# One-bank running sums, one decay tile per chunk, a later conversion of the first weights, and plain float32 second products for four pairs of the first tile

## The chip, the cores and the metric

The kernel runs on one core of a Trainium2 chip. The core has TensorE (PE in the profile; its weight loads are shown as PEld), VectorE (DVE), ScalarE (ACT), GpSimd (POOL) and SyncE (SP), which issues all DMAs here. The metric is the device time of one execution in microseconds; lower is better. A kernel's time is the median of its runs.

## The reference

Four sequences of 768 positions and 8 heads go through a state-space layer (chunks, a decaying state of 16 per head), and its output, 3072 tokens of 256 values, through two feed-forward layers:

```
for c in range(nc):                                  # chunks; cum = cumsum(log a)
    M = einsum(Cc, Bc) * exp(cum_i - cum_j) * causal
    y[c] = M @ xc + (Cc @ state) * exp(cum)
    state = exp(sum(la)) * state + sum_j Bx_j * exp(cum_last - cum_j)
x = y.transpose(0, 2, 1, 3).reshape(3072, 256)
h = x @ w_in                                         # 256 -> 2048
x = where(h > 0, h, exp(min(h, 0)) - 1) @ w_out      # 2048 -> 256
out = ((x @ w1) * (x @ w2)) @ w3 @ w_out2            # 256 -> 1024 -> 1024 -> 256
```

All is float32; the weights arrive as 64-bit words, of which the kernel makes float32 values.

## The kernel before, in words

**Tiles and units.** The 3072 tokens are six tiles of 512 (`t` = 0 to 5), each made of four chunks of 128 positions. For each tile there are 8 units `a` (`unit_a(t, n)`: the product `h` with `w_in`, two 512-column halves in one two-bank tile, then ELU on ACT and DVE, then a split into a rounded part and a remainder, `g`), 8 units `b` (`unit_b(t, n)`: `g` with `w_out`, summed over n in a tile `acc`), 8 units `c` (products with `w1` and `w2`, `ab`, multiplied on DVE into `p`) and 8 units `d` (`p` with `wp`, summed in `acc`). `wp` is w3 times the last weight, made once by 8 units `w`.

**Split products.** A product in full precision is three rounded products (float32r): `mm3` (lines 240 to 242) issues weight-remainder times value, weight times value-remainder, and weight times value. So each operand is held twice, and each value that feeds a product has a split (`split`, lines 103 and 104: a cast on ACT, a subtraction on DVE or POOL). The small products of the state-space chunks (lines 351, 387, 416, 422) use plain float32 operands; each of them stands in the trace as two MATMUL instructions.

**Pieces of weights.** `w_in` and `w_out` come in 8 pieces each. A piece has three stages: load (a DMA on SP's queue), bits (lines 146 to 148: two DVE instructions and one ACT instruction make float32 of the words, in place), parts (lines 103 and 104: the split into the stationary operands). The queue of pieces follows the order of the units that need them: entry 0 is `w_in`'s piece 0, then pieces 1 and 2, then entry 3 is `w_out`'s piece 0, and so on.

**Order.** The four chunks of tile 0 come first, each in four phases: prep (a scan on DVE, line 334, of the decay values that `at_wide` spreads over partitions by a product with a 0/1 matrix, line 321, then `bd` on POOL), cb (products and their decay, lines 351 and 359), state (cd on POOL, products line 387, states on DVE lines 396 and 399) and y (lines 416, 422, then x_made, lines 431 and 432). The list `ORDER` gives their order by hand: phase p of chunk k is number 4k + p; "pr" is a scan of the decays in another layout (lines 261 to 303), "aw" the second `at_wide`, "h" the first half of the columns of unit a(0, 0), and (i, s) takes entry i of the queue to stage s. The chunks of later tiles are set between the units of the tile before by a plan. Within the dependencies a scheduler at build time then fixes the order of each engine's instructions; every engine works through its own list in order.

**Rooms.** PSUM has eight banks of 512 float32. The pool `ps_w` has three rooms of two banks, `ps_a` one room of two banks, which holds `acc` (and `aw2` before). `xx` in SBUF has three rooms for each part of the tiles `xT` (input of a) and `x2` (output of b, input of c). x2 of tiles 0 to 2 is stored to DRAM and read back.

Of the kernel before, what the change touches and what calls it, by code (L numbers as in the profile page):

```python
# [7 lines left out]
F32 = mybir.dt.float32  # L8
F32R = mybir.dt.float32r
AF = mybir.ActivationFunctionType  # L10
ALU = mybir.AluOpType
# [8 lines left out]
TT = 512  # L20
NTILE = NB * S // TT
CPT = TT // Q
DM = NH * D
F1 = 2048
F2 = 1024
# [8 lines left out]
PACE, FOLD, LATE, END, FIRST = 1.5, 4.0, 12.0, 7.0, 8.0  # L34
SPILL, BACK = 3, 8

ORDER = [0, 4, 1, "pr", 2, "aw", (0, 2), 5, 3, 6, (0, 3), 8, 7, 9, (1, 2), 10, 12, 11, 13, (1, 3), 14, "h", 15, (2, 2), (3, 2)]


XCOLS = (("x", DM), ("bn", NH * N), ("bt", 2 * R), ("cz", 2 * 2 * R), ("cp", SUB * 2 * R))  # L40
# [3 lines left out]
def kernel(  # L44
# [21 lines left out]
    P = 128  # L66
# [35 lines left out]
    def split(hi, lo, raw, lo_eng):  # L102
        A.copy(hi, raw)  # L103
        return lo_eng.tensor_tensor(out=lo, in0=raw, in1=hi.bitcast(F32), op=ALU.subtract)  # L104

    def tmp(name):
        return act.tile([P, 2, TT], F32, tag="tmp", name=name, bufs=TMP)

    def banks(name):

        return ps_w.tile([P, 2, TT], F32, tag="w", name=name)
# [9 lines left out]
    class Piece:  # L121


        def __init__(self, name, src, room, dst):
            self.name, self.src, self.room, self.dst = name, src, room, dst
            self.done, self.lo = 0, G

        def advance(self, stage):
            while self.done < stage:
# [11 lines left out]
        def bits(self):  # L141

            low, high = self.low, self.high
            pace(V.tensor_scalar(low, low, 29, None, op0=ALU.logical_shift_right))
            pace(A.activation(high.bitcast(F32), high.bitcast(F32), AF.Prelu, scale=2.0 ** -112, alpha=2.0 ** 32))
            V.scalar_tensor_tensor(out=low, in0=high, scalar=3, in1=low,
                                   op0=ALU.logical_shift_left, op1=ALU.bitwise_or)

        def parts(self):
            hi, lo = self.dst()
            word = self.low.bitcast(F32)
            if isinstance(hi, list):
                for k in range(2):
                    split(hi[k], lo[k], word[:, k], self.lo)
            else:
                split(hi, lo, word, self.lo)
# [45 lines left out]
    def rows_of(ws):  # L204
        return lambda i: [w[:, 2 * i:2 * i + 2] for w in ws]

    def four(name, tag, shape):
        t = [wts.tile(shape, F32R, tag=f"{tag}_{j}", name=f"{name}_{j}") for j in range(4)]
        return [t[:2], t[2:]]
# [13 lines left out]
    def w3_dst(i):  # L223
# [9 lines left out]
        "w1": pieces_of("wa", cols(w1), w1_room, half_cols(w1_s, "w1")),  # L233
        "w2": pieces_of("wb", cols(w2), w2_room, half_cols(w2_s, "w2")),
    }

    last_mm = []

    def mm3(out, whi, wlo, xhi, xlo, first, last, **kw):
        last_mm[:] = [T.matmul(out, wlo, xhi, start=first, stop=False, **kw).ins]  # L240
        T.matmul(out, whi, xlo, start=False, stop=False, **kw)  # L241
        T.matmul(out, whi, xhi, start=False, stop=last, **kw)  # L242
# [72 lines left out]
    def at_wide(k):  # L315


        wide = ps_a.tile([P, 2, TT], F32, tag="acc", name=f"aw{k}") if k else banks(f"aw{k}")
        for j in range(2):
            for p in range(2):  # L320
                mm = T.matmul(wide[:, j], sel[:, k + j].rearrange("r s i -> r (s i)"),
                              cut[0][:, p].rearrange("r h i -> r (h i)"), start=p == 0, stop=p == 1)
                if j == p == 0:
                    tc.keep_in_program_order(mm)
            ck[k + j]["a"] = wide[:, j]

    def at_prep(k):

# [170 lines left out]

    early_h = []  # L500

    def products(h, t, n, cs):
        for j in range(2):
            fs = slice((2 * n + j) * P, (2 * n + j + 1) * P)
            for k in range(2):
                mm3(h[:, j, cs], w_in_s[0][:, k, fs], w_in_s[1][:, k, fs], xT[t][0][:, k, cs], xT[t][1][:, k, cs],
                    k == 0, k == 1)

    def first_half():

        early_h.append(banks("h0_0"))
        products(early_h[0], 0, 0, slice(0, TT // 2))

    def unit_a(t, n):

        early = early_h and (t, n) == (0, 0)
        h = early_h[0] if early else banks(f"h{t}_{n}")
        products(h, t, n, slice(TT // 2 if early else 0, TT))
        e = tmp(f"e{t}_{n}")
        A.activation(e, h, AF.Exp)  # L520

        A.activation(e, e, AF.Relu, scale=-1.0, bias=1.0)  # L522
        V.scalar_tensor_tensor(out=e, in0=e, scalar=-1.0, in1=h, op0=ALU.mult, op1=ALU.max)  # L523
        g = act.tile([P, 2, 2, TT], F32R, tag="g", name=f"g{t}_{n}")
        split(g[:, 0], g[:, 1], e, V)
        gt[t, n] = g

    def acc_of(key):
        if key not in accs:
            accs[key] = ps_a.tile([P, 2, TT], F32, tag="acc", name=f"acc_{key[0]}{key[1]}")  # L530
        return accs[key]

    def unit_b(t, n):
        acc = acc_of(("b", t))
        g = gt.pop((t, n))

        for i in range(2):
            es = slice(i * P, (i + 1) * P)
            for j in range(2):
                m = 2 * n + j  # L540
                mm3(acc[:, i], w_out_s[0][:, m, es], w_out_s[1][:, m, es], g[:, 0, j], g[:, 1, j], m == 0, m == F1 // P - 1)
        if m == F1 // P - 1:
            hi, lo = x2_of(t)
            for i in range(2):
                split(hi[:, i], lo[:, i], acc[:, i], V)
            if t < SPILL:
                for v, d in zip(x2.pop(t), x2_dram):
                    nc.sync.dma_start(d[t], v.bitcast(F32))

    x2_dram = [tc.dram_tile([SPILL, P, 2, TT], F32, name=f"x2_dram{p}") for p in ("h", "l")]  # L550

    def x2_of(t):
        if t not in x2:
            x2[t] = [act.tile([P, 2, TT], F32R, tag=f"xx{p}", name=f"x2{p}{t}", bufs=3) for p in ("h", "l")]
        return x2[t]
# [22 lines left out]
    def unit_d(t, m):  # L578
        acc = acc_of(("d", t))
        p = pt.pop((t, m))  # L580
        for i in range(2):
            es = slice(i * P, (i + 1) * P)
            mm3(acc[:, i], wp_s[0][:, m, es], wp_s[1][:, m, es], p[:, 0], p[:, 1], m == 0, m == F2 // P - 1)
        if m == F2 // P - 1:
            o = [tmp(f"o{t}")] * 2 if t < NTILE - 1 else [tmp(f"o{t}_{i}") for i in range(2)]
            A.copy(o[0][:, 0], acc[:, 0])
            V.tensor_copy(o[1][:, 1], acc[:, 1])
            for i in range(2):
                nc.sync.dma_start(outT[i * P:(i + 1) * P, t * TT:(t + 1) * TT], o[i][:, i])


    NA, NC = F1 // P // 2, F2 // P
# [124 lines left out]
        p.advance(1)  # L717
    for k in range(CPT):
        at_l(k)
    at_wide(0)  # L720
    for p in queue[:first_n]:
        p.lo = V

    for j in ORDER:
        if j == "pr":
            at_decay(0)
        elif j == "aw":
            at_wide(2)
        elif j == "h":
            first_half()  # L730
        elif isinstance(j, tuple):
            i, stage = j
            queue[i].advance(stage)
            if stage == 3:
                load_next(i)
        else:
            attn[j]()
            marks.extend(last_mm)
# [72 lines left out]
```

## Time and profile before

| | |
|---|---|
| time, median of 3 runs | 571.41 us (571.39 to 571.74) |
| the profiled execution's own time | 570.61 us |
| its span in the profile | 568.7 us |
| PE busy | 550.6 us, 97% of the span, 4436 matmuls |
| PE weight loads | 440.3 us, 77% |
| DVE busy | 337.0 us, 59% |
| ACT busy | 274.2 us, 48% |
| POOL busy | 85.8 us, 15% |

Busy time is the time in which at least one instruction of the engine was under way. Matmuls overlap (one starts before the one ahead of it has drained), so a stretch can be wholly busy and still hold fewer matmuls than it could: distances between starts tell more than the busy share. The shares are averages over stages that differ: the state-space chunks of tile 0 fill the first 28 us, the conversion of the first weights runs beside tile 0's units until about 76 us, and dense products fill the rest.

### The profile page before, as it was taken

Reading aid. Unit: us, or ns where it says so; the run is one execution under the profiler, and the core shown is the slowest. Engines: PE = TensorE matmul, PEld = TensorE weight load, DVE = VectorE, ACT = ScalarE, POOL = GpSimd, SP = SyncE. Lnnn points to the kernel's source line nnn. Section 1 sums busy time; section 2 is a strip of 40 time slices with the busy share of each in tenths; the row PEclk is TensorE's granted clock in tenths of the full one; section 3 lists DMA queues with packets and bytes.
Section 4 is the critical chain, followed back from the end, with each engine's and each line's share of the span. In section 5 each row is a group of like instructions: output and inputs, shape, how many; then the busy total and the mean of one; then the engine's idle time right before and its main releaser. Section 6 shows DMA issues by size and latency. Waiting matters only on the chain.

```text
span 568.7 us, 10514 instructions
## 1 busy us (share of the span) xinstructions
PE 550.6 (97%) x4436; PEld 440.3 (77%) x4436; DVE 337.0 (59%) x480; ACT 274.2 (48%) x378; POOL 85.8 (15%) x91
## 2 busy tenths in 40 slices
PE   5998999999999999999999999999999999999996
PEld 3676677878788888878787878877878878888785
DVE  6599987867878674757425434243766353344342
ACT  2297567567745566764214222223644452365232
POOL 2201112430333432351000000000111000000000
PEclk9999999999999999999999999999999999999999
DMA  8978352553434341640001511021000000010001
GB/s 289 324 254 242 133 165 80 168 183 112 149 111 150 131 157 67 222 136 12 0 1 39 192 50 56 2 93 56 37 20 2 2 1 0 1 37 0 1 0 38
DMA packets 27167, 52.78 MB, mean 93 GB/s; under 512 B 2192, under 2 KB 10384, under 8 KB 27120
## 3 DMA queue, kind: packets, MB, share of 16 engines
q1 hardware_dynamic: 27120, 52.11, 28.3%
q8 instruction: 35, 0.57, 0.4%
q14 instruction: 12, 0.10, 0.1%
HBM read 45.71 MB, written 6.39 MB: 92 GB/s over the span
## 4 chain that ended last, share of the span: by engine, by line
PE 84%; DVE 7%; issue 3%; DMA 2%; POOL 2%; ACT 1%; SPq 0%; DVEq 0%; POOLq 0%; ACTq 0%
PE ab L241 7%; PE ab L240 7%; PE ab L242 7%; PE h L240 7%; PE acc_b L242 6%; PE acc_b L240 6%; PE acc_b L241 6%; PE h L241 6%; PE h L242 6%; PE acc_d L240 4%; PE acc_d L241 4%; PE acc_d L242 4%; DMA raw_wa<-in_w 2%; PE s L351 2%; PE wp L240 1%
## 5 line engine op out<-in xcount | busy, mean ns | idle before, releaser
L104 DVE TENSOR_TENSOR g<-e,g 128x1024 fp32r<-128x1024 f32 x48 | 62.0, 1291 | 36.9 <-ACT g L103 36.5
L523 DVE SCALAR_TENSOR_TENSOR e<-e,h 128x1024 f32<-128x1024 f32 x48 | 58.4, 1216 | 38.9 <-ACT e L522 38.9
L240 PE MATMUL h<-xTh,w_in_lo 128*128 128x512 f32 (+1 forms) x196 | 77.6, 397 | 1.5 <-DVE pr L302 0.6
L241 PE MATMUL acc_b<-g,w_out_hi 128*128 128x512 f32 x192 | 75.3, 392 | 1.2 <-DVE g L104 1.2
L240 PE MATMUL acc_b<-g,w_out_lo 128*128 128x512 f32 x192 | 75.7, 394 | 0.6 <-DVE w_out_lo L104 0.3
L241 PE MATMUL h<-xTl,w_in_hi 128*128 128x512 f32 (+1 forms) x196 | 76.2, 389 | 0.0
L242 PE MATMUL h<-xTh,w_in_hi 128*128 128x512 f32 (+1 forms) x196 | 76.0, 388 | 0.0
L240 PE MATMUL ab<-x2h,w 128*128 128x512 f32 x192 | 74.3, 393 | 1.7 <-ACT x2h L103 1.4
L242 PE MATMUL acc_b<-g,w_out_hi 128*128 128x512 f32 x192 | 75.1, 391 | 0.0
L241 PE MATMUL ab<-x2l,w 128*128 128x512 f32 x192 | 74.9, 390 | 0.1
L242 PE MATMUL ab<-x2h,w 128*128 128x512 f32 x192 | 74.7, 389 | 0.0
L103 ACT CAST g<-e 128x1024 fp32r<-128x1024 f32 x48 | 50.6, 1055 | 42.7 <-DVE e L523 21.8
L569 DVE TENSOR_TENSOR pa<-pa,ab 128x512 f32<-128x512 f32 x48 | 32.7, 686 | 62.6 <-ACT pa L568 62.6
L520 ACT ACTIVATE e<-h 128x1024 f32<-128x1024 f32 x48 | 49.5, 1032 | 34.3 <-PE h L242 34.2
L568 ACT COPY pa<-ab 128x512 f32<-128x512 f32 x48 | 27.9, 588 | 78.8 <-PE ab L242 77.4
L104 DVE TENSOR_TENSOR p<-pa,p 128x512 fp32r<-128x512 f32 x48 | 32.8, 690 | 32.8 <-ACT p L103 32.5
L522 ACT ACTIVATE e<-e 128x1024 f32<-128x1024 f32 x48 | 51.4, 1070 | 0.9
L103 ACT CAST p<-pa 128x512 fp32r<-128x512 f32 x48 | 29.8, 621 | 39.4 <-PE acc_d L242 21.9
L240 PEld LDWEIGHTS h<-xTh,w_in_lo 128*128 128x128 f32 x196 | 37.2, 190 | 10.5 <-DVE pr L302 0.9
L240 PEld LDWEIGHTS ab<-x2h,w 128*128 128x128 f32 x192 | 35.9, 188 | 10.7 <-ACT x2h L103 2.3
L373 POOL TENSOR_TENSOR cd<-xbc,pr 128x256 f32<-128x256 f32 x24 | 24.7, 1029 | 124.9 <-PE s L422 110.6
L242 PEld LDWEIGHTS h<-xTh,w_in_hi 128*128 128x128 f32 x196 | 37.4, 191 | 7.5
(107 smaller groups left out, 901.2 us busy)
## 6 DMA issues: line engine op xcount, KB each, us to landing
xbc<-in_xc SPq DMA_DIRECT2D x24, 512.0 KB, 4.6
raw_wc<-in_w3t SPq DMA_DIRECT2D x16, 512.0 KB, 5.0
L<-a_cut SPq DMA_DIRECT2D x40, 128.0 KB, 4.6
raw_wi<-in_w_in SPq DMA_DIRECT2D x8, 512.0 KB, 6.1
raw_wo<-in_w_out SPq DMA_DIRECT2D x8, 512.0 KB, 6.1
out_t<-o SPq DMA_DIRECT2D x12, 256.0 KB, 2.0
raw_wq<-in_wo SPq DMA_DIRECT2D x4, 512.0 KB, 3.7
raw_wb<-in_w SPq DMA_DIRECT2D x4, 512.0 KB, 4.9
```

The source lines that it names most:

```text
L103: A.copy(hi, raw)
L104: return lo_eng.tensor_tensor(out=lo, in0=raw, in1=hi.bitcast(F32), op=ALU.subtract)
L240: last_mm[:] = [T.matmul(out, wlo, xhi, start=first, stop=False, **kw).ins]
L241: T.matmul(out, whi, xlo, start=False, stop=False, **kw)
L242: T.matmul(out, whi, xhi, start=False, stop=last, **kw)
L351: mm = T.matmul(cb[R * s:R * s + R, b, 2 * R * g:2 * R * g + 2 * R], c["bt"][rows, g], c["cz"][rows, g], start=True, stop=True, skip_group ...
L373: G.tensor_tensor(out=c["cd"], in0=c["cp"].rearrange("p s (w i) -> p s w i", w=2), in1=c["pr"].rearrange("p s (o i) -> p s o i", o=1).to_b ...
L520: A.activation(e, h, AF.Exp)
L522: A.activation(e, e, AF.Relu, scale=-1.0, bias=1.0)
L523: V.scalar_tensor_tensor(out=e, in0=e, scalar=-1.0, in1=h, op0=ALU.mult, op1=ALU.max)
L568: A.copy(e, h[:, 0])
L569: V.tensor_tensor(out=e, in0=e, in1=h[:, 1], op=ALU.mult)
```

## The change

Five things, all in the diff below.

1. `at_wide` makes the decay values of one chunk at a time, in a one-bank tile of its own (chunks 2 and 3 in the rooms `acc0` and `acc1`), not those of two chunks in a two-bank tile.
2. In `ORDER`, entry 0 of the queue is taken to stages 2 and 3, and entry 1 to stages 2 and 3, at later places; "h" is done in two parts, "h0" before and "h1" after the y phase of chunk 3.
3. The running sums `acc` of units b and d are two tiles of one bank, each with its own room, not one tile of two banks. The split of x2 and the copy of the output are issued for each half right after that half's last product. For half 0 the output copy now stands on DVE, for half 1 on ACT.
4. For tile 0 and n below 4 (`PLAIN`), unit b multiplies plain float32 operands: one `T.matmul` in place of `mm3`. The ELU's result goes straight into `g`, without a split. The bits stage of `w_out`'s pieces 0 to 3 writes its result into `words` (two tiles in the rooms `xx`), and their parts stage does nothing.
5. The split of these four pieces is done in unit a(1, n) instead, with the cast on ACT and the subtraction on DVE.

```diff
-ORDER = [0, 4, 1, "pr", 2, "aw", (0, 2), 5, 3, 6, (0, 3), 8, 7, 9, (1, 2), 10, 12, 11, 13, (1, 3), 14, "h", 15, (2, 2), (3, 2)]
+PLAIN = 4
+
+ORDER = ["a0", 0, "a1", 4, 1, "pr", 2, "a2", "a3", 5, 3, 6, (0, 2), 8, 7, 9, (0, 3), 10, 12, 11, 13, (1, 2), 14, "h0", (1, 3), 15, "h1",
+         (2, 2), (3, 2)]
...
@@ class Piece, bits and parts
-            V.scalar_tensor_tensor(out=low, in0=high, scalar=3, in1=low,
+            out = low if self.word is None else self.word().bitcast(U32)
+            V.scalar_tensor_tensor(out=out, in0=high, scalar=3, in1=low,
                                    op0=ALU.logical_shift_left, op1=ALU.bitwise_or)
 
         def parts(self):
+            if self.word is not None:
+
+                return
...
+    words = []
+
+    def word_of(n):
+
+        if not words:
+            words.extend(act.tile([P, 2, 2, DM], F32, tag=f"xx{p}", name=f"words_{p}", bufs=3) for p in ("h", "l"))
+        return words[n % 2][:, n // 2]
...
+    for n, p in enumerate(pc["w_out"][:PLAIN]):
+        p.word = lambda n=n: word_of(n)
...
@@ def at_wide(k)
-        wide = ps_a.tile([P, 2, TT], F32, tag="acc", name=f"aw{k}") if k else banks(f"aw{k}")
-        for j in range(2):
-            for p in range(2):
-                mm = T.matmul(wide[:, j], sel[:, k + j].rearrange("r s i -> r (s i)"),
-                              cut[0][:, p].rearrange("r h i -> r (h i)"), start=p == 0, stop=p == 1)
-                if j == p == 0:
-                    tc.keep_in_program_order(mm)
-            ck[k + j]["a"] = wide[:, j]
+        ck[k]["a"] = wide = ps_a.tile([P, TT], F32, tag=f"acc{k - 2}", name=f"aw{k}") if k > 1 else banks(f"aw{k}")[:, 0]
+        for p in range(2):
+            mm = T.matmul(wide, sel[:, k].rearrange("r s i -> r (s i)"),
+                          cut[0][:, p].rearrange("r h i -> r (h i)"), start=p == 0, stop=p == 1)
+            if p == 0:
+                tc.keep_in_program_order(mm)
...
-    def products(h, t, n, cs):
-        for j in range(2):
+    def products(h, t, n, cs, js=range(2)):
+        for j in js:
...
-        early_h.append(banks("h0_0"))
-        products(early_h[0], 0, 0, slice(0, TT // 2))
+        if j == 0:
+            early_h.append(banks("h0_0"))
+        products(early_h[0], 0, 0, slice(0, TT // 2), [j])
...
@@ def unit_a(t, n)
-        V.scalar_tensor_tensor(out=e, in0=e, scalar=-1.0, in1=h, op0=ALU.mult, op1=ALU.max)
-        g = act.tile([P, 2, 2, TT], F32R, tag="g", name=f"g{t}_{n}")
-        split(g[:, 0], g[:, 1], e, V)
+        plain = t == 0 and n < PLAIN
+        g = act.tile([P, 2, TT] if plain else [P, 2, 2, TT], F32 if plain else F32R, tag="g", name=f"g{t}_{n}")
+        elu = g if plain else e
+        V.scalar_tensor_tensor(out=elu, in0=e, scalar=-1.0, in1=h, op0=ALU.mult, op1=ALU.max)
+        if not plain:
+            split(g[:, 0], g[:, 1], e, V)
         gt[t, n] = g
+        if t == 1 and n < PLAIN:
+            split(*(w[:, 2 * n:2 * n + 2] for w in w_out_s), word_of(n), V)
 
     def acc_of(key):
+
         if key not in accs:
-            accs[key] = ps_a.tile([P, 2, TT], F32, tag="acc", name=f"acc_{key[0]}{key[1]}")
+            accs[key] = [ps_a.tile([P, TT], F32, tag=f"acc{i}", name=f"acc_{key[0]}{key[1]}_{i}") for i in range(2)]
         return accs[key]
...
@@ def unit_b(t, n)
-                mm3(acc[:, i], w_out_s[0][:, m, es], w_out_s[1][:, m, es], g[:, 0, j], g[:, 1, j], m == 0, m == F1 // P - 1)
-        if m == F1 // P - 1:
-            hi, lo = x2_of(t)
-            for i in range(2):
-                split(hi[:, i], lo[:, i], acc[:, i], V)
...
+                if t == 0 and n < PLAIN:
+                    last_mm[:] = [T.matmul(acc[i], word_of(n)[:, j, es], g[:, j], start=m == 0, stop=False).ins]
+                    continue
+                mm3(acc[i], w_out_s[0][:, m, es], w_out_s[1][:, m, es], g[:, 0, j], g[:, 1, j], m == 0, m == F1 // P - 1)
+            if m == F1 // P - 1:
+                hi, lo = x2_of(t)
+                split(hi[:, i], lo[:, i], acc[i], V)
...
@@ def unit_d(t, m)
-            mm3(acc[:, i], wp_s[0][:, m, es], wp_s[1][:, m, es], p[:, 0], p[:, 1], m == 0, m == F2 // P - 1)
-        if m == F2 // P - 1:
-            o = [tmp(f"o{t}")] * 2 if t < NTILE - 1 else [tmp(f"o{t}_{i}") for i in range(2)]
-            A.copy(o[0][:, 0], acc[:, 0])
-            V.tensor_copy(o[1][:, 1], acc[:, 1])
-            for i in range(2):
-                nc.sync.dma_start(outT[i * P:(i + 1) * P, t * TT:(t + 1) * TT], o[i][:, i])
+            mm3(acc[i], wp_s[0][:, m, es], wp_s[1][:, m, es], p[:, 0], p[:, 1], m == 0, m == F2 // P - 1)
+            if m == F2 // P - 1:
+                if i == 0 or t == NTILE - 1:
+                    o = tmp(f"o{t}_{i}")
+                (V.tensor_copy, A.copy)[i](o[:, i], acc[i])
+                nc.sync.dma_start(outT[i * P:(i + 1) * P, t * TT:(t + 1) * TT], o[:, i])
```

The call of `at_wide(0)` ahead of the loop over `ORDER` goes; "a0" to "a3", "h0" and "h1" call `at_wide(k)` and `first_half(j)` there.

## Rows read from the trace of the kernel before

**Rows 1.** The page, busy time of each engine over the whole span

```profile
PE 550.6 (97%) x4436; PEld 440.3 (77%) x4436; DVE 337.0 (59%) x480; ACT 274.2 (48%) x378; POOL 85.8 (15%) x91
```

**Rows 2.** Busy by stretch: length, PE, PEld, DVE, ACT, POOL, clock, DMA, GB/s

```profile
40.84:75.41 34.57, 31.40 (x457) 23.08 (x456) 34.04 (x53) 23.38 (x32) 5.70 (x8) 1.00 0.57 177
83.80:126.21 42.41, 42.41 (x525) 33.23 (x524) 32.96 (x47) 26.89 (x33) 13.35 (x11) 1.00 0.43 144
...
461.00:530.00 69.00, 69.00 (x306) 57.08 (x304) 27.34 (x31) 28.71 (x35) 0.00 (x0) 1.00 0.02 8
```

**Rows 3.** The same stretches, instructions of line 240 alone (one mm3 each): PE, PEld

```profile
40.84:75.41 34.57, 13.08 (x32) 6.00 (x32) 1.00 0.57 177
83.80:126.21 42.41, 19.72 (x50) 9.26 (x50) 1.00 0.43 144
```

**Rows 4.** Matmul groups by form, whole span: busy us, mean ns of one

```profile
L242 PE MATMUL acc_b<-g,w_out_hi 128*128 128x512 f32 x192 | 75.1, 391 | 0.0
...
L351 PE MATMUL s<-xbc 32*64 32x128 f32 x320 | 14.8, 281 | 0.0
...
L416 PE MATMUL s<-L,xbc 64*32 64x64 f32 x480 | 9.4, 222 | 0.0
```

**Rows 5.** Timeline of the start: start us, duration us, what, idle before

```profile
4.21 2.36 PE L321 MATMUL aw<-a_hl,sel 8*128 8x512 f32 x4 [4.21 <-ACT a_hl L103]
...
6.61 2.34 DVE L334 TENSOR_TENSOR_SCAN L<-aw,eye 128x512 f32<-128x512 f32 x2 [1.74 <-PE aw L321]
...
9.78 0.42 DVE L146 TENSOR_SCALAR raw_wi<-raw_wi 128x512 uint32<-128x512 uint32 x1
...
10.45 0.68 DVE L148 SCALAR_TENSOR_TENSOR raw_wi<-raw_wi 128x512 uint32<-128x512 uint32 x1
...
11.19 1.22 DVE L303 TENSOR_TENSOR_SCAN pr<-pr,begun 128x512 f32<-128x512 f32 x1
```

**Rows 6.** Timeline, end of the chunks of tile 0

```profile
24.27 0.41 PE L242 MATMUL h<-xTh,w_in_hi 128*128 128x256 f32 x1
...
27.53 0.62 PE L240 MATMUL h<-xTh,w_in_lo 128*128 128x256 f32 x2 [0.49 <-ACT xTh L431]
...
28.69 0.28 PE L240 MATMUL h<-xTh,w_in_lo 128*128 128x256 f32 x1
```

**Rows 7.** Timeline, the wait ahead of unit a(0, 2)

```profile
32.44 0.47 PE L240 MATMUL h<-xTh,w_in_lo 128*128 128x512 f32 x1 [0.35 <-DVE w_in_lo L104]
```

**Rows 8.** Groups of DVE and ACT from 27 to 75.41 us

```profile
L104 DVE TENSOR_TENSOR g<-e,g 128x1024 fp32r<-128x1024 f32 x7 | 8.7, 1244 | 0.0
...
L104 DVE TENSOR_TENSOR w_out_lo<-raw_wo,w_out_hi 128x512 fp32r<-128x512 f32 x6 | 4.1, 680 | 0.0
...
L103 ACT CAST g<-e 128x1024 fp32r<-128x1024 f32 x7 | 7.7, 1099 | 1.7 <-PE acc_b L242 0.9 <-DVE e L523 0.8
...
L103 ACT CAST w_out_hi<-raw_wo 128x512 fp32r<-128x512 f32 x7 | 5.0, 709 | 5.8 <-DVE raw_wo L148 5.8
```

**Rows 9.** Timeline where units b end and c begin, tiles 4 and 5

```profile
457.30 0.39 PE L242 MATMUL acc_b<-g,w_out_hi 128*128 128x512 f32 x1
...
460.01 0.50 PE L241 MATMUL ab<-x2l,w 128*128 128x512 f32 x1
...
529.93 0.39 PE L242 MATMUL acc_b<-g,w_out_hi 128*128 128x512 f32 x1
...
530.36 0.58 ACT L103 CAST x2h<-acc_b 128x512 fp32r<-128x512 f32 x1 [4.38 <-PE acc_b L242]
...
530.99 0.97 PE L240 MATMUL ab<-x2h,w 128*128 128x512 f32 x3 [0.68 <-ACT x2h L103]
...
531.70 0.59 ACT L103 CAST x2h<-acc_b 128x512 fp32r<-128x512 f32 x1 [0.76 <-DVE x2l L104]
```

**Rows 10.** Timeline of the end

```profile
564.25 0.58 ACT L586 COPY o<-acc_d 128x512 f32<-128x512 f32 x1 [2.30 <-PE acc_d L242]
...
564.87 0.69 DVE L587 COPY o<-acc_d 128x512 f32<-128x512 f32 x1 [2.19 <-ACT o L586]
```

More of the change, by code (lines that the diff above doesn't have):

```diff
@@ L125, in __init__ @@
             self.name, self.src, self.room, self.dst = name, src, room, dst
-            self.done, self.lo = 0, G
+            self.done, self.lo, self.word = 0, G, None
         def advance(self, stage):
@@ L507, in products, with first_half @@
                     k == 0, k == 1)
-    def first_half():
-        early_h.append(banks("h0_0"))
-        products(early_h[0], 0, 0, slice(0, TT // 2))
+    def first_half(j):
+        if j == 0:
+            early_h.append(banks("h0_0"))
+        products(early_h[0], 0, 0, slice(0, TT // 2), [j])
     def unit_a(t, n):
@@ L540, in unit_b @@
                 m = 2 * n + j
-                mm3(acc[:, i], w_out_s[0][:, m, es], w_out_s[1][:, m, es], g[:, 0, j], g[:, 1, j], m == 0, m == F1 // P - 1)
-        if m == F1 // P - 1:
-            hi, lo = x2_of(t)
-            for i in range(2):
-                split(hi[:, i], lo[:, i], acc[:, i], V)
-            if t < SPILL:
-                for v, d in zip(x2.pop(t), x2_dram):
-                    nc.sync.dma_start(d[t], v.bitcast(F32))
+                if t == 0 and n < PLAIN:
[5 more added lines that the diff above has]
+                split(hi[:, i], lo[:, i], acc[i], V)
+        if m == F1 // P - 1 and t < SPILL:
+            for v, d in zip(x2.pop(t), x2_dram):
+                nc.sync.dma_start(d[t], v.bitcast(F32))
     x2_dram = [tc.dram_tile([SPILL, P, 2, TT], F32, name=f"x2_dram{p}") for p in ("h", "l")]
@@ L719 @@
         at_l(k)
-    at_wide(0)
     for p in queue[:first_n]:
@@ L726 @@
             at_decay(0)
[L727 to L730, printed above, removed]
+        elif j in ("a0", "a1", "a2", "a3"):
+            at_wide(int(j[1]))
+        elif j in ("h0", "h1"):
+            first_half(int(j[1]))
         elif isinstance(j, tuple):
```

## The prediction

> **What bounds the kernel.** I read the page first: PE is busy for 97% of the span [rows 1]. A busy share says nothing of density, so the second view is a stretch that holds nothing but rounded 512-column products: from 461 to 530 us there are 304 weight loads, one for each product, in 69.00 us [rows 2], so one starts every 0.227 us while each lasts 0.39 [rows 9]. That step is the price of one product, and three of them, 0.68 us, that of an mm3.
>
> The third view sets two stretches side by side. From 40.84 to 75.41 us (chunks of tile 1 beside units of tile 0) there are 32 mm3, from 83.80 to 126.21 us (chunks of tile 2 beside units of tile 1) 50 [rows 3]. Their products take 96 x 0.227 = 21.8 us and 150 x 0.227 = 34.0 us; the rest of the stretches, 34.57 - 21.8 = 12.8 us and 42.41 - 34.0 = 8.4 us, holds the small products of four chunks each, and waits [rows 2, 3]. The same chunks cost 4.4 us more in the first. There DVE is busy 34.04 of 34.57 us, in the second 32.96 of 42.41 [rows 2]. So PE waits for DVE while the first weights are converted, and nowhere for long after it. One more wait of that kind, 0.5 us beyond the normal step, lies ahead of a(0, 2) [rows 7]. In all about 4.9 us of PE time is lost beside tile 0.
>
> Three other losses are short: the start until about 28 us, where PE works in bursts [rows 5, 6]; the places where c follows b directly [rows 9]; and the end [rows 10].
>
> **The change, part by part.**
>
> *Decay tiles.* The four spreading products run from 4.21 to 6.57 us and the first scan begins at 6.61, after the last of them, although it reads only what the first two make [rows 5]. Two of the four at an even pace would end near 5.4, 1.2 us earlier; as the second also waits for its operand's subtraction on DVE, I take 0.9, a start near 5.7. cb of chunk 0 and both scans follow on engines that are free. Gain 0.9 us on DVE's list; bounds 0 (if something later gates) and 1.2.
>
> *Later conversion.* DVE's two bits instructions of entry 0, 0.42 and 0.68 us, stand ahead of the pr scan at 11.19 [rows 5], on which cd (POOL) and the first y depend. Moved behind u of chunk 1 they leave that path, but fall on the DVE list of chunks 2 and 3, where entry 1's conversion stood; that in turn moves behind cb of chunk 3, its parts behind h0. Nothing is saved in total, so I count about half of the 1.1 us: 0.5. Its ACT instructions lie beside free ACT time at this stage. The loads they release (entries 8 and 9, SP's queue) start later by as much, and are needed some 20 us after. Bounds 0 and 1.1.
>
> *h in two parts.* Now twelve 256-column products stand ahead of the last y, and after y PE waits 0.49 us for xTh and then needs 0.62 for two products, as xTl is late too [rows 6]. With six of the twelve behind y, PE has some 1.3 us of work (six steps of 0.21, 256 columns at 1.2 GHz) while ACT and DVE make xT. Gain 0.8 us; bounds 0.5 (that one wait) and 1.2.
>
> The start together: -2.2 us, between -0.5 and -3.5.
>
> *Plain products: PE.* Before, the trace shows no plain 512-column product. It shows plain ones of 128 and 64 columns, two instructions each (320 at line 351 for 20 chunks of 8 products): 281 and 222 ns, so 59 ns for 64 columns, 0.92 ns a column; a rounded one steps 0.227 us for 512, 0.44 ns a column [rows 2, 4]. So each of the two instructions passes its columns twice, four passes for a product: 4 x 0.227 = 0.91 us, by the slope 2 x 512 x 0.92 = 0.94 us. As a lower bound two passes without the step's overhead at the large form, 0.88 us. A mm3 is 0.68. I take 0.91: +0.23 for each of 4 pairs x 4 products = +3.6 us, bounds 3.2 and 4.2. Going from one kind to the other costs up to 0.1 us of unhidden weight load (a first product after a wait lasts 0.50 as against 0.39 [rows 9]): 8 switches, 0 to 0.8, taken 0.4. Together +4.0 us.
>
> *Plain products: DVE and ACT.* Beside tile 0 DVE loses four subtractions of g at 1.24 us and four of w_out at 0.68, 7.7 us; ACT four casts of g at 1.10 and four of w_out at 0.71, 7.2 us [rows 8]. About 1.4 us of DVE comes back in this stretch with the first two splits in a(1, n). DVE's 34.04 us then become some 28 in a stretch of about 34, a share of 0.82, as in the second stretch (0.78), which I take as the measure of no waits [rows 2]. Of 4.9 us of waits I expect 0.9 to stay: -4.0 us, bounds 0 and -4.9. So the plain products pay for themselves on PE and no more: PE takes over as the bound of this stretch, net 0.0, between -1.7 and +5.0.
>
> *The four late splits.* 4 x 0.68 us on DVE and 4 x 0.71 on ACT go into tile 1's units, where DVE has 9.4 and ACT 15.5 us free in 42 [rows 2, 8]; that is the cover. Behind a late split stand the ELU of the next unit and the scan of the next chunk, for which PE's b and s wait. I count +0.3; without the cover +2.7. The tiles `words` hold one of three `xx` rooms until the fourth split, and x2 of tile 0 and xT of tiles 1 and 2 take the other two in turn; x2 is now made earlier by a half, so I count no wait.
>
> *One-bank sums, b to c.* In tile 5 the last b product starts at 529.93; the next could at 530.16 and starts at 530.99. ACT casts half 0 at 530.36, only after half 1's products, and half 1 at 531.70 after DVE has subtracted half 0 [rows 9]. With a tile per half, half 0 (done six products or 1.4 us earlier) is split under half 1's products: the 0.83 us goes, and 0.2 of slow steps behind it. In tile 4 PE has from 457.30 to 460.01, 2.71 us, in which four steps of 0.23 fit (457.30 and three c products): 1.8 us lost [rows 9]. DVE has other work queued there, an ELU among it, so I count 1.2. Together -2.2 us; bounds 0 and -2.8.
> The two casts wait for each other though the halves lie in two banks. The Trainium skill (PSUM — Partial Sum Buffer, section PSUM bank collisions raise a hardware error) says that engines collide within one bank and quadrant and run clean on different banks. By that rule the wait in the trace comes from the tile, and the sum stands; by the row alone the second half might wait again, and this term would be 0.
>
> *The end.* The copy of half 1 (DVE, 0.69) waits for that of half 0 (ACT, 0.58) [rows 10]. Now half 0 is copied under half 1's products, and the last copy is ACT's at 564.25: its DMA goes at 564.83 where it went at 565.56. -0.7 us; bounds 0 and -0.75.
>
> Sum: -2.2 + 0.0 + 0.3 - 2.2 - 0.7 = -4.8 us. The profiled execution took 570.61 us, of which 1.9 lie around its span; it would be 565.8. The median is 0.8 above the profiled one, so 571.41 - 4.8 = **566.6 us**.
>
> **Rivals.**
>
> 1. *The waits beside tile 0 stay.* They would be chains (scan, POOL, PE) and not DVE's load. For it: a scan cannot move up past what its engine's list has ahead of it. Against it: tile 2's chunks have the same chains and not the waits. +4.0: 570.6 us, about as before.
> 2. *The halves don't part.* ACT and DVE are busy with other things when half 0 is ready, or the waits come from elsewhere. The terms of b to c and of the end fall away: +2.9, 569.5 us.
> 3. *The start doesn't carry.* POOL and the y chain gate chunks 2 and 3 whatever DVE does: +2.2, 568.8 us.
> 4. *TensorE's clock, the slower side.* At 24.27 us a 256-column product lasts 0.41 us, at 28.69 it lasts 0.28 [rows 6]: the 0.13 less fits a rise from 1.2 to 2.4 GHz (256 columns take 0.21 and 0.11 us), though the column of granted clock, third from the end, prints 1.00 in every stretch that I asked for [rows 2]. Ahead of 24 us PE had worked in bursts, ahead of 28.7 with little pause but the one at 27.5. If h1 behind y and shorter bursts put the rise off, each 512-column product at the lower level costs 0.2 us more, a plain one 0.9. From 24 rounded products, a(0, 0) and a(0, 1), the gain of 4.8 us is gone; with the first plain pair as well it is 575 us. Against it: h1 fills a gap, it opens none, and the gaps from 40 to 75 us did not bring the lower level back.
> The Trainium skill (TensorE: Matmul & The Clock Gate, Part 1) has the lower level as the state after idleness and the upper one after sustained work; the trace agrees in direction, and by that rule fuller work lets the clock rise no later.
> 5. *The late splits hurt.* +2.4: 569.0 us.
>
> **How the numbers follow.** Forecast 0.58 (its own range 564.8 to 568.4, from halves of the bounds above); rival 1 0.13, rival 2 0.10, rival 3 0.11, rival 4 0.05, rival 5 0.03. Two of 1, 2, 3 and 5 together reach 571 and beyond. 0.2% of the time, 1.1 us, is about what a measurement can tell from no change: 570.3 to 572.6 is the same. Faster: forecast, 2, 3, 5, and a part of 1 (waits that go halfway): 0.85. The same: the rest of 1 and doubles, 0.09. Slower: rival 4 and a wait not thought of, 0.06. The range of 8 in 10 takes in rivals 2, 3 and 5 above, and below the start's and the waits' full bounds (-1.3 and -1.7): 563.6 to 570.0.
>
> **What the profile after would show.** First scan near 5.7 us and pr scan near 9.5; the last y of tile 0 near 24.5 and products without a gap behind it; unit b(0, 0) with 8 plain instructions at lines of `unit_b`, some 0.45 us apart; in the stretch of tile 1's chunks DVE below 0.9 busy; ACT's x2h of half 0 under half 1's products in tiles 4 and 5; the last copy on ACT, with the span's end 4.4 - 0.7 us after the last product's. The prediction is wrong if plain products step over 0.5 us, if b of tile 0 waits as before, or if x2h of half 0 still begins after half 1's last product.

## The result, and the profile after

The changed kernel took **567.26 us** (median of 4, 565.6 to 568.31) where the kernel before took 571.58 beside it (4, 571.39 to 572.91): a ratio of 0.991 [0.9884, 0.9935], 4.3 us less. Measured again among the experiments it took 565.71 us, 0.9894 [0.9881, 0.9907]. The forecast, 566.6, lies between the two. The profiled execution took 567.03 us with a span of 564.9, 3.8 less than the span before.

The page of the changed kernel, busy time of each engine, answers to [rows 1]: 16 matmuls and 4 DVE and 4 ACT instructions fewer, and the same 97% of PE.

```profile
PE 549.5 (97%) x4420; PEld 437.3 (77%) x4420; DVE 332.9 (59%) x476; ACT 271.0 (48%) x374; POOL 83.6 (15%) x91
```

A share of 97% on both sides tells nothing of where 3.8 us went. For that the same product is looked up in both traces, and the lengths between such places are set side by side:

| stretch | before | after | difference |
|---|---|---|---|
| start, to the first product behind the last y of tile 0 | 27.53 | 27.83 | +0.30 |
| from there to a(0, 7), the last unit a of tile 0: a and b of tile 0 beside chunks of tile 1 | 47.88 | 46.31 | -1.57 |
| to the third unit c | 184.54 | 185.41 | +0.87 |
| from the third to the 32nd unit c (c and d of four tiles) | 134.77 | 132.97 | -1.80 |
| to the last unit c of tile 4 | 89.19 | 89.19 | 0.00 |
| to the last unit d of tile 5 | 78.53 | 77.52 | -1.01 |
| to the end of the span | 6.25 | 5.65 | -0.60 |

The sum is -3.8 us. The predicted terms were -2.2 for the start, 0.0 and +0.3 around tile 0, -2.2 where b ends, -0.7 at the end, and nothing for the fourth row. So the total was near and most of the terms were not.

**The start.** The timeline of the changed kernel, answering to [rows 5, 6]:

```profile
5.79 2.34 DVE L350 TENSOR_TENSOR_SCAN L<-aw,eye 128x512 f32<-128x512 f32 x2 [0.88 <-PE aw L338]
...
9.43 1.23 DVE L321 TENSOR_TENSOR_SCAN pr<-pr,begun 128x512 f32<-128x512 f32 x1
...
11.17 0.70 PE L367 MATMUL cb<-xbc 32*64 32x128 f32 x8 [1.11 <-DMA xbc<-in_xc]
...
19.04 0.68 PE L432 MATMUL y<-L,xbc 64*32 64x64 f32 x32 [1.62 <-DVE L L375]
...
25.43 0.41 PE L260 MATMUL h<-xTh,w_in_hi 128*128 128x256 f32 x1
25.78 0.98 PE L432 MATMUL y<-L,xbc 64*32 64x64 f32 x32
...
27.83 0.62 PE L258 MATMUL h<-xTh,w_in_lo 128*128 128x256 f32 x2 [0.49 <-ACT xTh L447]
```

The first scan starts 0.82 us earlier and the pr scan 1.76, as predicted (5.7, 9.5). Then PE stands at 11.17 for chunk 1's data, a transfer, and at 19.04 for a decay on DVE, and what was won is gone. All twelve early products still stand ahead of the last y (the first at 22.92, the last at 25.43), so the 0.49 us wait for xTh at 27.83 is the old one.

**Beside tile 0.** Stretches of the kernel before and of the changed one (columns as in [rows 2]):

```profile
27.53:75.41 47.88, 44.36 (x516) 33.35 (x516) 47.35 (x74) 36.69 (x51) 5.70 (x8) 1.00 0.67 207
```
```profile
27.83:74.14 46.31, 45.80 (x501) 30.49 (x501) 43.79 (x73) 33.35 (x47) 5.52 (x8) 1.00 0.70 219
40.80:74.14 33.34, 33.34 (x452) 21.96 (x450) 30.82 (x50) 20.68 (x29) 4.64 (x7) 1.00 0.60 191
```

DVE falls from 47.35 of 47.88 us (0.99) to 43.79 of 46.31 (0.95). What a plain product costs is read from the timeline of one unit, and from the view of line 565 alone (ns: least, median, most):

```profile
35.90 3.70 PE L565 MATMUL acc_b<-g,words_h 128*128 128x512 f32 x8 [0.17 <-DVE g L543]
39.04 0.79 PE L258 MATMUL h<-xTh,w_in_lo 128*128 128x512 f32 x1
39.67 0.39 PE L259 MATMUL h<-xTl,w_in_hi 128*128 128x512 f32 x1
```
```profile
L565 PE MATMUL acc_b<-g,words_h x16: 590/592/697, 35.9 to 54.4; 128*128 128x512 f32 x16
```

From 35.90 to 39.67 lie eight plain instructions and one rounded (0.23). The first plain one lasts 697 ns where the others last 592, 0.10 us more. The rest is (3.77 - 0.23 - 0.10) / 8 = 0.43 us each, 0.86 for a product. The 0.10 is no price of entering: it stands where the group follows a wait (35.90) or small products (43.15, 53.88, 59.50), while the group at 49.46, directly behind rounded products, begins with 590 ns. The 0.79 at 39.04 looks like a price of leaving; it is the last plain instruction still running under it, as the sum shows.

**Where b ends, and the end.** The timeline of the changed kernel at tile 4, at tile 5 and at the last copies, answering to [rows 9, 10]:

```profile
455.09 0.39 PE L260 MATMUL acc_b<-g,w_out_hi 128*128 128x512 f32 x1
455.61 1.06 ACT L106 CAST x2h<-acc_b 128x512 fp32r<-128x512 f32 x2
455.93 1.21 DVE L543 SCALAR_TENSOR_TENSOR e<-e,h 128x1024 f32<-128x1024 f32 x1
...
457.06 1.28 DVE L107 TENSOR_TENSOR x2l<-acc_b,x2h 128x512 fp32r<-128x512 f32 x2
...
527.01 0.59 ACT L106 CAST x2h<-acc_b 128x512 fp32r<-128x512 f32 x1 [3.25 <-PE acc_b L260]
...
527.63 0.69 DVE L107 TENSOR_TENSOR x2l<-acc_b,x2h 128x512 fp32r<-128x512 f32 x1 [2.62 <-ACT x2h L106]
527.72 0.39 PE L260 MATMUL acc_b<-g,w_out_hi 128*128 128x512 f32 x1
...
527.95 0.84 PE L258 MATMUL ab<-x2h,w 128*128 128x512 f32 x3
528.15 0.59 ACT L106 CAST x2h<-acc_b 128x512 fp32r<-128x512 f32 x1 [0.54 <-PE acc_b L260]
...
560.36 0.69 DVE L612 COPY o<-acc_d 128x512 f32<-128x512 f32 x1 [0.91 <-PE acc_d L260]
560.39 0.39 PE L260 MATMUL acc_d<-p,wp_hi 128*128 128x512 f32 x1
560.87 0.59 ACT L612 COPY o<-acc_d 128x512 f32<-128x512 f32 x1 [2.15 <-PE acc_d L260]
```

In tile 5 half 0 is cast at 527.01, under half 1's products, and c starts at 527.95, one step of 0.23 behind the last b product: the gap is gone. Half 1 is cast from 528.15 while DVE still subtracts half 0 (527.63 + 0.69 = 528.32). The Trainium skill (PSUM — Partial Sum Buffer, section PSUM bank collisions raise a hardware error) has engines run clean on different banks; these two rows agree. In tile 4 nothing changed: both casts begin at 455.61, after all of b, and an ELU stands ahead of both subtractions on DVE. At the end the copies overlap: the last ends at 561.46, 1.07 us behind the start of the last product, where it was 565.56 - 563.76 = 1.80.

### The profile page after: what moved, and what is told of

Read it like the earlier page. It is cut to its first block, busy times and chain, and to the rows that moved or that the text cites. A ratio compares the mean times of both kernels' runs of the same rounds, so it can differ in the third digit from the quotient of the medians.

```text
span 564.9 us, 10467 instructions
## 1 busy us (share of the span) xinstructions
PE 549.5 (97%) x4420; PEld 437.3 (77%) x4420; DVE 332.9 (59%) x476; ACT 271.0 (48%) x374; POOL 83.6 (15%) x91
## 4 chain that ended last, share of the span: by engine, by line
PE 89%; DMA 3%; DVE 3%; issue 2%; POOL 1%; ACT 1%; SPq 0%; DVEq 0%; POOLq 0%; ACTq 0%
PE ab L260 8%; PE ab L259 8%; PE ab L258 7%; PE h L258 7%; PE h L259 7%; PE h L260 7%; PE acc_b L258 6%; PE acc_b L259 6%; PE acc_b L260 6%; PE acc_d L258 4%; PE acc_d L259 4%; PE acc_d L260 4%; PE acc_b L565 3%; PE s L367 2%; DMA raw_wa<-in_w 2%
## 5 line engine op out<-in xcount | busy, mean ns | idle before, releaser
L543 DVE SCALAR_TENSOR_TENSOR e<-e,h 128x1024 f32<-128x1024 f32 x44 | 53.6, 1217 | 45.7 <-ACT e L539 41.0
L258 PE MATMUL h<-xTh,w_in_lo 128*128 128x512 f32 (+1 forms) x196 | 78.9, 403 | 0.9 <-ACT xTh L447 0.5
L107 DVE TENSOR_TENSOR g<-e,g 128x1024 fp32r<-128x1024 f32 x44 | 55.4, 1260 | 31.5 <-ACT g L106 31.4
L259 PE MATMUL acc_b<-g,w_out_hi 128*128 128x512 f32 x176 | 68.9, 391 | 1.3 <-DVE g L107 1.3
L260 PE MATMUL acc_b<-g,w_out_hi 128*128 128x512 f32 x176 | 68.8, 391 | 0.0
L258 PE MATMUL acc_b<-g,w_out_lo 128*128 128x512 f32 x176 | 66.9, 394 | 0.0
L106 ACT CAST g<-e 128x1024 fp32r<-128x1024 f32 x44 | 46.2, 1049 | 36.2 <-DVE e L543 20.3
L259 PEld LDWEIGHTS h<-xTl,w_in_hi 128*128 128x128 f32 x196 | 37.4, 191 | 7.8 <-issue 1.0
```

Source lines behind the costliest of these rows:

```text
L543: V.scalar_tensor_tensor(out=elu, in0=e, scalar=-1.0, in1=h, op0=ALU.mult, op1=ALU.max)
```

## The experiments

Three parts alone first, and the changed kernel again beside them. Theory: the parts' gains add up to the whole. Rivals: the gain is all in one part, or parts need each other. The edits are shown against the changed kernel, cut to the lines that matter.

**One-bank sums alone** (start and products as before):

```diff
-PLAIN = 4
...
-ORDER = ["a0", 0, "a1", 4, 1, "pr", 2, "a2", "a3", 5, ...]
+ORDER = [0, 4, 1, "pr", 2, "aw", (0, 2), 5, 3, 6, ...]
...
```


> One-bank sums alone, all else as before. Theory A (read from the changed kernel's trace: the sums give 1.0 us where b of tile 5 ends and 0.6 at the end, and nothing where b of tile 4 ends): 1.6 us less than before, 570.0. Theory B (as predicted: the end of b in tile 4 gives 1.2 more): 2.8 less, 568.8. Theory C (the sums also reorder the units d beside tile 4's chunks and so give the 1.6 us that the changed kernel gained there): 3.2 less.

569.4 us, 0.9957 [0.9942, 0.9972]. Its trace has the changed kernel's three gains (132.97 us from the third to the 32nd unit c, 77.52 to the last d, 5.61 to the end) and, like it, none where b of tile 4 ends (89.19): theory C.

**Plain products alone** (two-bank sums, start as before):

```diff
-            accs[key] = [ps_a.tile([P, TT], F32, tag=f"acc{i}", ...) for i in range(2)]
+            accs[key] = ps_a.tile([P, 2, TT], F32, tag="acc", ...)
...
```


> Plain second products and words alone, all else as before. Theory A (the waits beside tile 0 go, some 6.5 us, and the plain products cost PE about 5): 1 to 2 us less than before, about 570. Theory B (predicted: nothing net): 571.5. If the plain products cost more than the waits: above 572.6.

571.89 us, 1.0012 [0.9989, 1.0036]: nothing, and executions from 570.21 to 577.98 us, the profiled one 574.1. The six whose mean granted clock is 0.998 or more took 570.21 to 572.17, the six at 0.997 or less 571.6 to 577.98. Its timeline in chunk 6, and the stretch right after:

```profile
58.13 0.34 PE L404 MATMUL s<-xbc,bd 64*32 64x64 f32 x16
60.88 0.68 PE L433 MATMUL s<-L,xbc 64*32 64x64 f32 x32 [2.40 <-DVE L L376]
```
```profile
60.70:64.05 3.35, 3.17 (x66) 2.11 (x67) 1.94 (x5) 2.74 (x4) 0.87 (x1) 0.50 0.24 91
```

PE waits 2.4 us for a decay that DVE makes behind other work, and then the granted clock is at its lower level for 3.4 us. In the changed kernel's trace chunk 6 has no such wait.

**The start alone** (a decay tile per chunk, the new order, h in two parts; chunks 2 and 3 share a two-bank room):

```diff
+        aw_room.append(ps_a.tile([P, 2, TT], F32, tag="acc", name="aw23"))
...
-        plain = t == 0 and n < PLAIN
...
```


> Decay tile per chunk, later conversion and h in two parts alone (chunks 2 and 3 share one two-bank room). Theory A (the start doesn't carry: the second chunk's data and the y chain gate it): within 0.5 us of before. Theory B (predicted): 2.2 us less, 569.3, with the first dense product of tile 0 near 25.5 us and not 27.5.

571.55 us, 0.9998 [0.9987, 1.0009]: nothing. Here the start did carry: the product of 27.53 before stands at 26.14, 1.39 us earlier. But a(0, 7) starts 0.38 earlier only, a(3, 7) 0.20, and the third unit c 0.25 later. The stretch beside tile 0, bound by DVE, took 1.0 of it. The three executions with a mean granted clock of 0.999 or 1.0 took 571.4 to 571.75, so no fall of the clock hides a gain.

**The changed kernel again.**

> The changed kernel once more. Median 567.3 within 0.7. If the second chunk's data landed late in its first profile by chance, its landing near 11.0 us moves to near 10.0 in this one, and h0 with it from 22.9 to about 22; if it is the order of the queue, it stays near 11.0.

565.71 us, 0.9894. Chunk 1's data stayed late: POOL's bd, which reads them, began at 10.85 us (11.16 in the first trace), and h0 at 22.61. The three parts alone give -2.5, +0.7 and -0.1 us (ratios times 571.9): they don't add up, parts need each other. Two pairs of parts tell which.

**Sums and plain products, start as before:**

```diff
-ORDER = ["a0", 0, "a1", 4, 1, "pr", 2, "a2", "a3", 5, ...]
+ORDER = [0, 4, 1, "pr", 2, "aw", (0, 2), 5, 3, 6, ...]
...
-    def products(h, t, n, cs, js=range(2)):
-        for j in js:
+    def products(h, t, n, cs):
+        for j in range(2):
...
```


> The changed kernel with the order of the start as before (decay tiles, conversion, h in one part). Theory A (the start is worth nothing by itself, but with the plain products it keeps PE from the 2.75 us wait for chunk 6 that the plain products alone ran into): slower than the changed kernel, 568 to 570. Theory B (what the sums and the plain products give simply adds up: 2.5 and 0): 569.4 with a quiet stretch from 30 to 75 us. Theory C (the start is not needed): 565.7, as the changed kernel.

568.41 us, 0.9952 [0.993, 0.9973]: slower than the changed kernel's 0.9894, as theory A has it; theory B's time lies within the interval too.

**Sums and start, no plain products:**

```diff
-PLAIN = 4
+PLAIN = 0
```


> The changed kernel without plain products (all products of tile 0 in three rounded ones, weights split as before). Theory A (the sums give 2.5, the start alone nothing, since DVE then holds tile 0's units back): 569.4. Theory B (the start gives its 2 us and the plain products nothing): 567.

567.83 us, 0.9929 [0.9912, 0.9947]. Sums alone were at 0.9957, both pairs lie a little below that, and all three at 0.9894. Start and plain products each brought little alone; together, beside the sums, 0.0063 or 3.6 us (2.7 by the changed kernel's first ratio, 0.991). In the trace without plain products the stretch from the last y to a(0, 7) takes 48.80 us (27.07 to 75.87), 0.92 more than before: a head start ends at DVE's list. In that of sums and plain products it takes 47.02 with a wait of 1.07 us in chunk 6, where the changed kernel has none and takes 46.31.

**h1 held behind the last y on PE.** Theory: the start fails since PE's order puts h1 ahead of y.

```diff
+        for y in behind:
+            tc.add_manual_dep(last_mm[0], y.name, ...)
...
```


> The changed kernel with h1 held behind the last y of tile 0 on PE, as its ORDER lists it; in the changed kernel's trace the scheduler had put it ahead of y. As predicted: y ends some 1.3 us earlier, PE's wait of 0.5 for xT is covered: 0.8 us less than the changed kernel. Theory A (behind the start DVE is the bound until 60 us, so a gain there is absorbed): 0 to 0.4 less.

567.36 us, 0.9914 [0.9887, 0.994], 564.6 to 569.83: not clear of the changed kernel. The product of 27.53 before came at 26.00, 1.54 us earlier. But chunk 6's wait was back in the profiled execution, the slowest of the six (a stretch and two timeline rows of it):

```profile
60.60:63.90 3.30, 3.30 (x5) 1.35 (x4) 2.27 (x3) 2.54 (x4) 0.51 (x1) 0.50 0.59 220
```
```profile
59.17 0.46 PE L435 MATMUL s<-L,xbc 64*32 64x64 f32 x32 [2.40 <-DVE L L378]
...
60.13 4.54 PE L573 MATMUL acc_b<-g,words_l 128*128 128x512 f32 x6
```

Six plain instructions take 4.54 us where eight took 3.70. So an earlier start isn't enough by itself: it must not land in that wait.

**Chunk 1's load ahead of the first weights' load.** Theory: chunk 1's data gate the start.

```diff
+    at_load(1)
     queue[0].advance(1)
-    for k in range(1, CPT):
+    for k in range(2, CPT):
```


> The changed kernel with chunk 1's load issued ahead of the first weights'. Its data landed at 10.7 to 11.0 us, after DVE's pr scan had begun, and cb of chunk 1 waited 1.1 us for it. If that landing gates the start: landing near 9.5, cb near 9.8, h0 some 1 us earlier, and up to 1 us less in all. If the chain of DVE and y gates it: h0 within 0.3 of the changed kernel's.

564.87 us, 0.9878 [0.9857, 0.9898]. Two rows of its timeline, for those at 11.17 and 27.83 of the changed kernel:

```profile
10.19 1.13 PE L367 MATMUL cb<-xbc 32*64 32x128 f32 x16
...
26.28 0.61 PE L258 MATMUL h<-xTh,w_in_lo 128*128 128x256 f32 x2 [0.49 <-ACT xTh L447]
```

cb of chunk 1 no longer waits for a transfer, the last y and its successor come 1.55 us earlier, and a(0, 7) starts at 72.58 (74.14): the head start carries through. The changed kernel's second trace had 26.91 and 73.23, and the next kernel, with the same start, 26.66 and 72.98, so the edit is worth 0.25 to 1.6 us there; the ratios of this kernel and the changed one overlap.

**The same, and the ELU of a(5, 1) behind x2's split of tile 4:**

```diff
+        if (t, n) == (NTILE - 1, 1):
+            behind(relu, x2_casts)
+            behind(made, x2_subs)
...
```


> The kernel with chunk 1's load first, and with the ELU of unit a(5, 1) (its second ACT and its DVE instruction) held behind x2's split of tile 4. In every trace so far PE loses 1.7 us where b of tile 4 ends, and DVE does that ELU (1.22 us) ahead of x2's subtraction. Theory A (other work in DVE's and ACT's lists keeps the halves from being split at once): 1.0 to 1.6 us less than chunk 1's load first alone, 563.5, and the gap there falls from 1.7 to under 0.6. Theory B (the wait is one on rooms of PSUM, which that ELU frees): no gain or a loss.

564.24 us, 0.9868 [0.9851, 0.9885], the lowest median of all, though its interval overlaps that of one experiment back. Its timeline at tile 4:

```profile
453.10 0.59 ACT L580 CAST x2h<-acc_b 128x512 fp32r<-128x512 f32 x1
...
453.53 0.39 PE L260 MATMUL acc_b<-g,w_out_hi 128*128 128x512 f32 x1
...
453.76 0.71 PE L258 MATMUL ab<-x2h,w 128*128 128x512 f32 x2
...
455.11 0.50 PE L259 MATMUL ab<-x2l,w 128*128 128x512 f32 x1 [0.65 <-DVE x2l L581]
```

Half 0 is now cast under half 1's products. From the first to the last unit c of tile 4 nothing moves, but that first unit comes 0.85 us earlier than in the kernel one experiment back (453.76 for 454.61), and the stretch from the 32nd unit c to the last of tile 4 falls from 89.21 to 88.29: 0.9 of the term predicted as 1.2, of which a 0.65 us wait for DVE stays.

**The late splits forced behind the ELU of a(1, n).**

```diff
+            behind(A.copy(hi, word_of(n)), [relu])
+            behind(V.tensor_tensor(out=lo, ...), [made])
...
```


> The changed kernel with the splits of w_out's pieces 0 to 3 held behind the ELU of units a(1, 0) to a(1, 3), where the code lists them; in the changed kernel's trace the scheduler had put them back beside tile 0, from 30.8 us on. As predicted: DVE has 2.7 us less beside tile 0 and PE's 0.34 us wait ahead of a(0, 2) goes: 0.3 to 1 us less than the changed kernel. Theory A (beside tile 0 PE is the bound already, and tile 1 gets the load): within 0.5 of it, and the stretch of tile 1's units longer by up to 1 us.

565.65 us, 0.9886 [0.9868, 0.9903]: the same as without it (0.9894). The subtractions now stand at 87.4 to 106.4 us, and the wait ahead of a(0, 2) is gone.

**Plain products for two pairs:**

```diff
-PLAIN = 4
+PLAIN = 2
```


> The changed kernel with two plain pairs in place of four. Theory A (each pair takes about 1.7 us of waits off PE's path and costs PE 1.2): half way between no plain pair (567.8) and four (565.7 to 567.3): about 567. Theory B (the first two take all the waits, the others only cost PE): 1 to 2 us under the changed kernel. Theory C (it hangs on the scheduler's order around chunk 6: a wait of 2.5 us there and the clock at half for 3.4 us): 568 or more.

566.75 us, 0.9911 [0.9896, 0.9926], between none (0.9929) and four (0.9894), as theory A has it, though the intervals overlap. The stretch from the last y to a(0, 7) takes 46.58 us, where it took 48.80 with no pair and 46.31 with four.

## Why the prediction was right, and which of its steps failed

The time was right because errors cancelled. By the signs that the prediction gave for being wrong, it was wrong in tile 4, where x2h of half 0 still begins after half 1's last product.

**The start (-2.2 predicted, +0.30 in the profiled execution) failed.** The first step is in "Later conversion": moved, the instructions "fall on the DVE list of chunks 2 and 3", and yet half of their time was counted as won. In the changed kernel the last of them stands directly ahead of chunk 2's decay (L375), for which PE's y waits at 19.04; the kernel before for comparison:

```profile
17.34 1.04 DVE L107 TENSOR_TENSOR w_in_lo<-raw_wi,w_in_hi 128x512 fp32r<-128x512 f32 x1 [0.53 <-ACT w_in_hi L106]
...
18.31 0.68 DVE L375 TENSOR_TENSOR L<-cb,L 128x512 f32<-128x512 f32 x1
```
```profile
19.05 0.68 PE L416 MATMUL y<-L,xbc 64*32 64x64 f32 x32 [0.53 <-DVE L L359]
```

PE's products u of chunk 2 still came 1.10 us earlier than before (16.96 for 18.06); at this y the lead is gone. The wait is 1.48 to 1.62 us in all nine traces with the new order and 0.53 in the four with the old one. No run put the conversion back by itself, so its price in time is not shown.

The second step is "h in two parts": PE did not get that order, and holding h1 behind y moved the stage, so the order was worth something. The third is chunk 1's transfer. With the order of loads unchanged, bd of chunk 1 began at 9.86 to 11.59 us in eleven traces, at 11.16 in this one and at 10.09 in the one before, so a part of the +0.30 is bad luck: the changed kernel's second trace is 0.6 ahead of before (26.91). In the four traces of the new order in which bd began by 10.1 us (the start alone, h1 behind y, and the two with chunk 1's load first), the product of 27.53 stood at 26.00 to 26.66. So this is rival 3 with other gates than it named, and 0.9 to 1.5 of the 2.2 us were there. Where the start came early without the plain products, nothing was won, since the next stage was DVE's.

**Plain products (net 0.0 predicted, -1.57 in the stage).** The view was right: DVE bound this stage, and all pairs together moved the bound to PE. The sizes: a product takes 0.86 us, not 0.91, so 16 of them cost 16 x (0.86 - 0.68) = +2.9, not +3.6, and less than the lower bound of 3.2. Going from one kind to the other costs nothing that these rows show. Time in that stretch outside the large products fell from 13.7 to 9.3 us (lengths less 0.2275 for each rounded 512-column instruction, 0.117 for each of 256, 0.43 for each plain one): -4.4, where waits of -4.0 and switches of +0.4 had been counted. PE's waits of the stretch (total us, times, longest), the four largest before and all of them after:

```profile
PE s L387 <- POOL bd L340: 1.3, 2, 0.7
PE h L240 <- DVE pr L302: 0.6, 1, 0.6
PE h L240 <- ACT xTh L431: 0.5, 1, 0.5
PE s L422 <- DVE st L396: 0.5, 1, 0.5
```
```profile
PE h L258 <- ACT xTh L447: 0.5, 1, 0.5
PE h L258 <- DVE w_in_lo L107: 0.3, 1, 0.3
PE acc_b L565 <- DVE g L543: 0.2, 1, 0.2
```

Rival 1 is ruled out: the chain waits (POOL, st) left as DVE's list got shorter, and with sums and start alike the time outside the large products is 14.6 us with no pair, 11.0 with two and 9.3 with four. But with other orders of the same work another wait comes, that for DVE's decay in chunk 6, and it decides whether the gain is seen. Which edit puts DVE's decay of chunk 6 late was not isolated.

**The late splits (+0.3) were not late.** The timeline of the changed kernel, DVE beside a(0, 1):

```profile
32.50 0.68 DVE L107 TENSOR_TENSOR w_out_lo<-words_h,w_out_hi 128x512 fp32r<-128x512 f32 x1
```

They are emitted in a(1, n) and read nothing that is late, so the order on the engines has the four subtractions at 32.50, 34.04, 44.02 and 49.41, and the 0.34 us wait of [rows 7] stays. Forcing them late gained nothing that could be measured, so rival 5's +2.4 us was not there either way.

They are not why DVE was 0.92 busy from 40.8 us on, where the prediction had 0.82: the two that fall in this stretch are the 1.4 us that it had allowed. The step that failed is "DVE's 34.04 us then become some 28". It took all eight subtractions, 7.7 us, off a stretch that begins at 40.84, but in the kernel before three of them lie ahead of it, at 32.21, 34.88 and 36.42:

```profile
32.21 0.68 DVE L104 TENSOR_TENSOR w_out_lo<-raw_wo,w_out_hi 128x512 fp32r<-128x512 f32 x1
...
36.42 1.22 DVE L104 TENSOR_TENSOR g<-e,g 128x1024 fp32r<-128x1024 f32 x1
```

The five others took 5.2 us, and 34.04 - 5.2 + 1.4 is 30.2, near the 30.82 measured. The waits went all the same, so a share of 0.82 was not needed for that.

**One-bank sums.** Tile 5 gave -1.0 as predicted, the end -0.6 of 0.7. Tile 4 gave 0 of 1.2, the step "DVE has other work queued there, an ELU among it, so I count 1.2": not DVE alone but ACT's Relu and DVE's ELU both went first, and holding them back gave 0.9. That is half of rival 2, and it could be had. What was missed outright is the fourth row of the table. The same number of instructions, in the kernel before and the changed one:

```profile
259.96:394.73 134.77, 134.77 (x901) 106.67 (x900) 57.80 (x93) 38.79 (x66) 5.45 (x8) 1.00 0.14 47
```
```profile
259.55:392.52 132.97, 132.97 (x901) 106.82 (x900) 57.83 (x93) 39.27 (x66) 5.36 (x8) 1.00 0.14 47
```

and in detail, a chunk of tile 4 beside units c and d, before and after:

```profile
276.37 0.65 PE L351 MATMUL s<-xbc 32*64 32x128 f32 x12
276.95 0.49 PE L240 MATMUL acc_d<-p,wp_lo 128*128 128x512 f32 x1
277.38 0.43 PE L351 MATMUL s<-xbc 32*64 32x128 f32 x4
```
```profile
278.68 0.67 PE L367 MATMUL s<-xbc 32*64 32x128 f32 x16
...
279.55 0.50 PE L258 MATMUL acc_d<-p,wp_lo 128*128 128x512 f32 x1
```

Before, a chunk's small products are cut by single large ones; after, they stand together. Counted over the stretch, PE goes 30 times between small and large products in the kernel before and in the two others without the new sums, which take 134.77 to 134.81 us for it, and 20 times in all ten with them, which take 132.97. The same sums cost 0.74 us from a(0, 7) to a(3, 7) when alone (167.80 us for 167.06, with 30 switches for 28), most of the third row's +0.87. That the new sums do this is shown; that the switches are the cause is not. The counts would make it some 0.18 us each in the first stretch and 0.37 in the second, and no run changed them alone.

**Rival 4, the clock.** In the changed kernel's two traces the lower level did not come back. It did in five profiled executions of other kernels, each time beside waits of PE (below): for 3.4 us in or just ahead of this stage in four, and for 6.8 us (18.06 to 24.89) in that of the start alone. The pair of traces leaves something out here. The traces with a fall have a mean granted clock of 0.993 to 0.997, the others 0.999 or 1.0. By that mark most executions of the kernel before had one: it was at 0.995 to 0.997 in 42 of the 51 executions beside the experiments, which took 572.0 us on average; the nine others, at 0.998 or more, took 571.2. Its profiled execution (1.0) is of the rarer kind. Of the changed kernel's eight executions one was at 0.997, its slowest (568.31). So some 0.5 us of the difference between the medians goes with the clock, with the opposite sign to rival 4's, and it helped the forecast: the profiled executions differ by 3.6 us. Of the executions whose clock is on record, 57 of 75 without plain products were at 0.997 or less, and 3 of 39 with plain products and the new sums (that with h1 behind y, 3 of 6, left out). Shorter waits beside tile 0 would explain that; no run isolates it.

## What to carry to other kernels

Before counting a saving at the start or ahead of a bound stage, look what the next stage waits for: here 1.4 us won at the start were worth nothing until the engine that bound the next stage had been relieved, and the other way round. A split of a tile frees an engine only if its instructions are also put first in that engine's list, so look up what stands ahead of them there. And compare the stretches that a change should leave alone as well: the largest gain of one part lay in one of them.

## What the runs showed of the hardware

- Where PE's products of chunk 6 stood 2.7 us apart (58.13 to 60.88 us with plain products alone, 56.43 to 59.17 with h1 behind y) the granted clock then fell to 0.50, that is 1.2 GHz, for 3.4 us. Where they stood 1.42 us apart (58.00 to 59.42, sums and plain products) it did not. Shorter waits in quick succession were followed by a fall too: of 1.19 us ahead of 49.99 and 0.80 ahead of 52.28, with the fall at 51.97 (sums and start), of 0.89 and 0.49 us ahead of 28.55 (late splits forced, whose profiled execution was its slowest, 568.13 us), of 1.48 us ahead of 17.70 with the fall at 18.06 (the start alone). At the lower level a plain instruction steps 0.85 us. The Trainium skill (TensorE: Matmul & The Clock Gate, Part 1) has the lower level as the state after idleness; these traces agree in direction.
- A plain float32 product of 512 columns takes two instructions of 0.43 us, each near the 0.45 us of two rounded products (2 x 0.227). The first of a group lasted 0.10 us longer behind a wait or small products, and no longer directly behind rounded products.
- The same program's first product behind the last y of tile 0 stood at 27.83 and at 26.91 us in two executions, with POOL's bd of chunk 1, which waits for a transfer, at 11.16 and 10.85 us: this start varies by as much as an edit to it brings.
